# First routing and last convolution in two-bank units with a hand-placed order, and half of the casts on ScalarE

## The chip, the cores and the metric

The kernel runs on one core of one Trainium2 chip. The metric is the time of one execution on the device in microseconds (us); lower is better. The other engines are named as in the profile: PE is TensorE, PEld its weight loads, DVE is VectorE, ACT is ScalarE, POOL is GpSimd, SP the engine that issues most transfers. One run of the kernel before (547.71 us) was slow and is left out of the ratios of its job. PSUM is where this kernel's matmuls leave their results, in banks of 512 columns, and an eviction is a copy out of it by VectorE or ScalarE. A half-clock window is a stretch in which the records show a TensorE clock of 0.50.

## The reference, cut to what matters

Clustered attention feeds a gated convolution. Every key and query row is assigned to the nearest of 16 centroids of its head, a query attends only to keys of its own cluster, and the result goes through a projection into three parts, a circular convolution over the sequence (a multiplication of spectra) and an output projection.

```python
# q, k, v: (4, 8, 768, 64); centroids: (8, 16, 64)
q_assign = np.argmax(np.einsum('bhsd,hcd->bhsc', q_n, c_n), axis=-1)   # k_assign the same from k_n
mask = q_assign[:, :, :, None] == k_assign[:, :, None, :]
scores = np.where(mask, scale * np.matmul(q, k.transpose(0, 1, 3, 2)), -1e9)
attn = softmax(scores)                                   # cut: written out in the reference
x = np.matmul(attn, v).transpose(0, 2, 1, 3).reshape(4, 768, 512)
proj = x @ w_proj                                        # 512 -> 1536
x1, x2, x3 = np.split(proj, 3, axis=-1)
x2_conv = irfft(rfft(x2, axis=1) * rfft(filter_fft, axis=0), axis=1)
out = (x1 * x2_conv * x3) @ w_out
```

## The kernel before

The program has three stages.

- **Head.** The first group of four heads is loaded and transposed on PE, its similarities to the centroids are computed, and an argmax on VectorE gives one-hot rows. These are written into the operand tiles of the scores (`aug`) by small transfers. Before the first group can be used, tables of sines for the Fourier transform are built too: angles on VectorE, sines on ScalarE.
- **Loop.** 96 steps. Each step computes two score tiles on PE, two exps on ScalarE, values on PE in fp32, and two running sums on VectorE. Between these, a list called `lead` prepares the routing of the next group, and a list called `conv` runs the convolution of the batch before, one "unit" at a time.
- **Tail.** The convolution of the last batch, with no attention left to hide it.

The parts that the change touches, with cuts marked:

```python
# PSUM: eight banks. psS: two tiles of two banks, psO: one of two, psF: two of one.
def bank():                        # one bank at a time; in head and tail also halves of psS
    ...

def forward_tables(m):             # angles on VectorE, called inside routing(0) between the casts
    nc.vector.scalar_tensor_tensor(n, kc, sm, sh, op0=Alu.mult, op1=Alu.add)
    nc.vector.tensor_scalar(r, n, 1.0 / S, MAGIC, op0=Alu.mult, op1=Alu.add)
    nc.vector.tensor_scalar(r, r, MAGIC, -float(S), op0=Alu.subtract, op1=Alu.mult)
    nc.vector.tensor_tensor(n, n, r, op=Alu.add)

def tables():                      # runs as the first units of the loop
    ...                            # loads flo, fhi of the filter from ScalarE's queue
    for j in range(6):             # inverse tables: PE transposes, ScalarE copies
        ...
    nc.vector.tensor_tensor(fu, flo, fhi, op=Alu.add)
    nc.vector.tensor_tensor(fd, flo, fhi, op=Alu.subtract)
    ...                            # filter spectrum into hm, all products on VectorE

def routing(n):
    ...
    (nc.gpsimd if n else nc.vector).tensor_copy(augs[aset][0][:D, z], qf[:D])
    nc.gpsimd.tensor_copy(augs[aset][1][D:, z], qf[D:])
    if n == 0 and z:
        forward_tables(z - 1)
    ...                            # similarities, argmax, scatter

def store(self, x32):              # attention output of a pair of heads
    nc.vector.tensor_tensor(uT[:, 0, kt], x32[:, :, :64], x32[:, :, 64:], op=Alu.add)
    nc.vector.tensor_tensor(uT[:, 1, kt], x32[:, :, :64], x32[:, :, 64:], op=Alu.subtract)
    nc.gpsimd.tensor_copy(xT[:, kt], x32[:].rearrange("p t c -> p (t c)"))

def hyena(b, xT, uT, last=False):
    ...
    # convolve: one bank per half spectrum, 512 wide
    for cs in range(2):
        ps = spectrum(i, cs, uv2[:, 0], uv2[:, 1])
        for r in range(2):
            nc.vector.tensor_tensor(tm[r][:, cs], ps, hm[:, i, 2 * r + cs], op=Alu.mult)
        for r in range(2 if cs else 0):
            (nc.vector if last and r else nc.gpsimd).tensor_tensor(
                y[:, i, r], tm[r][:, 0], tm[r][:, 1], op=Alu.add)
    # invert: sum and difference on VectorE, gate product alternately on GpSimd and VectorE
    # expand: output projection, 512 wide, one transfer for two row tiles

drain(routing(0)); forward_sines()     # the sines come behind the scatter
...
while conv and paid[0] + 0.3 < due:    # fills the step with convolution units
    unit(conv)
```

The softmax here doesn't subtract the row's maximum and nothing guards it: scores larger than these inputs give would overflow.

Of the kernel before, what the change touches and what calls it, by code (L numbers as in the profile page):

```python
# [30 lines left out]
def kernel(  # L31
# [29 lines left out]


    spare = []
    more_banks = [0]

    def bank():
        if spare:
            return spare.pop(0)
        if more_banks[0]:
            more_banks[0] += 1  # L70
            if more_banks[0] % 4 in (0, 2):
                w = psS.tile([128, 2, 512], F32, name="ps")
                spare.append(w[:, 1])
                return w[:, 0]
        return psF.tile([128, 512], F32, name="pf")[:]
# [33 lines left out]
    ident = consts.tile([128, 128], F32)  # L109
    make_identity(nc, ident)  # L110
    for z in range(4):
        load_qk(0, z // 2, z % 2, (nc.sync, nc.scalar)[z % 2])
    load_v(0, 0)
    identb = consts.tile([128, 128], BF16)
    nc.vector.tensor_copy(identb, ident)
    ones32 = consts.tile([128, 32], F32)
    nc.gpsimd.memset(ones32, 1.0)

    cbd = consts.tile([128, 4, 32], F32)
    nc.gpsimd.memset(cbd, 0.0)  # L120
    cen = ctx.enter_context(tc.tile_pool(name="cen", bufs=1))
    c = cen.tile([128, D], F32)
    nc.gpsimd.dma_start(c, centroids.rearrange("h c d -> (h c) d"))
    c2 = cen.tile([128, D], F32)
    nc.vector.tensor_tensor(c2, c, c, op=Alu.mult)
    ss = cen.tile([128, 1], F32)
    nc.vector.tensor_reduce(ss, c2, axis=AX, op=Alu.add)
    nc.vector.tensor_scalar(ss, ss, 1e-30, None, op0=Alu.max)
    s0 = cen.tile([128, 1], F32)
    nc.scalar.activation(s0, ss, Act.Sqrt)  # L130

    s1 = cen.tile([128, 1], F32)
    nc.vector.reciprocal(s1, s0)
    nc.vector.tensor_tensor(s1, s1, ss, op=Alu.mult)
    nc.vector.tensor_tensor(s1, s1, s0, op=Alu.add)
    nc.vector.tensor_scalar(s1, s1, 0.5, 1e-6, op0=Alu.mult, op1=Alu.add)
    nc.vector.reciprocal(s1, s1)
    cn = cen.tile([128, D], F32)
    nc.vector.tensor_scalar(cn, c, s1, None, op0=Alu.mult)
    cps = bank()  # L140
    nc.tensor.transpose(cps[:D, :128], cn, ident)
    cv = cps[:D, :128].rearrange("d (r e c) -> d r e c", r=4, e=2)
    nc.vector.tensor_copy(cbd[:D, :, :NC], cv[:, :, 0])
    nc.vector.tensor_copy(cbd[D:, :, NC:], cv[:, :, 1])


    mka = consts.tile([128, 1], F32)
    mkb = consts.tile([128, 1], F32)
    for g in range(4):
        nc.gpsimd.memset(mka[32 * g:32 * g + 32], BIG if g % 2 == 0 else 1.0)  # L150
        nc.gpsimd.memset(mkb[32 * g:32 * g + 32], -BIG if g % 2 == 0 else 0.0)

    revc = consts.tile([128, 48, NC], BF16)
    nc.gpsimd.iota(revc, pattern=[[0, 48], [-1, NC]], base=NC, channel_multiplier=0,
                   allow_small_or_imprecise_dtypes=True)



    NSET = 2
    augs = [[consts.tile([128, 4, S], BF16, name=f"aug{i}{hp}") for hp in range(2)] for i in range(NSET)]  # L160
    nc.gpsimd.memset(augs[0][1][:D], 0.0)


    NP = 6
    pbuf = [consts.tile([128, S + 4], F32, name=f"p{i}") for i in range(NP)]
    for p in pbuf:
        nc.gpsimd.memset(p[:, S:S + 1], EPS)
    np_ = [0]

    wpj = consts.tile([128, ND, 3 * DM], BF16)  # L170
    wout = consts.tile([128, ND, DM], BF16)

# [3 lines left out]
    hw = ctx.enter_context(tc.tile_pool(name="hw", bufs=1))  # L176


    fw = [consts.tile([128, 3, HS], BF16, name=f"fw{i}") for i in range(2)]
    inv = consts.tile([128, 6, HS], BF16)  # L180
    hm = consts.tile([128, 3, 4, DM], BF16)
# [14 lines left out]
    def forward_tables(m):  # L196
        MAGIC = 12582912.0
        if m < 3:
            sm = cen.tile([128, 1], F32)
            nc.vector.tensor_scalar(sm, sq, float(2 * m), None, op0=Alu.add)  # L200
            n, r = (pbuf[2 * m + i][:, :S].rearrange("p (a b) -> p a b", a=2) for i in range(2))
            nc.vector.scalar_tensor_tensor(n, kc, sm, sh, op0=Alu.mult, op1=Alu.add)
            nc.vector.tensor_scalar(r, n, 1.0 / S, MAGIC, op0=Alu.mult, op1=Alu.add)
            nc.vector.tensor_scalar(r, r, MAGIC, -float(S), op0=Alu.subtract, op1=Alu.mult)
            nc.vector.tensor_tensor(n, n, r, op=Alu.add)

    def forward_sines():
        for m in range(3):
            n = pbuf[2 * m][:, :S].rearrange("p (a b) -> p a b", a=2)
            for i in range(2):  # L210
                nc.scalar.activation(fw[i][:, m], n[:, i], Act.Sin, scale=2.0 * math.pi / S)

    def tables():

        flo = hy.tile([128, 3, DM], F32, name="hy")
        fhi = hy.tile([128, 3, DM], F32, name="hy")
        fv = moe_filter_fft.rearrange("(w p m e) d -> w e p m d", w=2, p=64, m=3, e=2)
        for e in range(2):
            nc.scalar.dma_start(flo[64 * e:64 * e + 64], fv[0, e])
            nc.scalar.dma_start(fhi[64 * e:64 * e + 64], fv[1, e])  # L220

        for j in range(6):
# [10 lines left out]
            yield 0.3  # L233
        fu = hw.tile([128, 3, DM], BF16, name="x3", bufs=2)
        fd = hw.tile([128, 3, DM], BF16, name="x3", bufs=2)
        nc.vector.tensor_tensor(fu, flo, fhi, op=Alu.add)
        nc.vector.tensor_tensor(fd, flo, fhi, op=Alu.subtract)

        w1 = cen.tile([128, 1], F32)
        wz = cen.tile([128, 1], F32)  # L240
        wv = cen.tile([128, 1], F32)
        nc.gpsimd.memset(wz, 2.0 / S)
        nc.gpsimd.memset(wz[0:1], 0.0)
        nc.gpsimd.memset(wv, 2.0 / S)
        nc.gpsimd.memset(wv[0:1], 1.0 / S)
        nc.gpsimd.memset(w1, 0.0)
        nc.gpsimd.memset(w1[0:1], 1.0 / S)
        for i in range(3):
            for cs in range(2):
                ps = spectrum(i, cs, fu, fd)  # L250
                w = (wv, wz)[cs] if i == 0 else 2.0 / S
                nc.vector.tensor_scalar(hm[:, i, 2 * cs], ps, w, None, op0=Alu.mult)
# [8 lines left out]
            nc.vector.tensor_scalar(hm[:, i, 1], hm[:, i, 2], -1.0, None, op0=Alu.mult)  # L261

    def spectrum(i, cs, fu, fd):

        ps = bank()
# [13 lines left out]
    def routing(n):  # L279
        aset, g = n % NSET, n % 2  # L280
        qkT = {}
        for pr in range(2):
            for j in range(2):
                qr = qk_raws.pop((n, pr, j))
                z = 2 * pr + j
                qkT[z] = rt.tile([128, 2, 384], F32, name="qkT", bufs=4)
                for ch in range(2):
                    tps = bank()
                    for t in range(3):
                        nc.tensor.transpose(tps[:, ts(t, 128)],  # L290
                                            qr[:, 3 * ch + t].rearrange("p h d -> p (h d)"), ident)
                    nc.scalar.copy(qkT[z][:, ch], tps[:, :384])  # L292
                    if ch == 1:
                        load_qk(n + 1, pr, j)
                    yield 0.38
                qf = qkT[z][:].rearrange("p a b -> p (a b)")
                (nc.gpsimd if n else nc.vector).tensor_copy(augs[aset][0][:D, z], qf[:D])  # L297
                nc.gpsimd.tensor_copy(augs[aset][1][D:, z], qf[D:])
                if n == 0 and z:
                    forward_tables(z - 1)  # L300
        sim = rt.tile([128, 2, 384], F32, name="sim")
        for ch in range(2):
            sim_ps = bank()
            for z in range(4):
                nc.tensor.matmul(sim_ps[32 * z:32 * z + 32, :384], cbd[:, 2 * g + z // 2],
                                 qkT[z][:, ch], start=True, stop=True)
            nc.scalar.copy(sim[:, ch], sim_ps[:, :384])
            yield 0.75
        mx = rt.tile([128, 2, 24], F32, name="mx")
# [44 lines left out]
    class Pair:  # L354
# [110 lines left out]
        def store(self, x32):  # L465
# [3 lines left out]
            nc.gpsimd.tensor_copy(xT[:, kt], x32[:].rearrange("p t c -> p (t c)"))  # L469


    def hyena(b, xT, uT, last=False):
        uvf = uT[:].rearrange("p e k t c -> p e k (t c)")
        uv2 = hy.tile([128, 2, 3, DM], BF16, name="hy")
        y = hy.tile([128, 3, 2, DM], BF16, name="hy")
        y2 = hy.tile([128, ND, S], BF16, name="hy")
        gate = {}

        def project():
            for m in range(3):  # L480
                for e in range(2):
                    ps = bank()
                    for kt in range(ND):
                        nc.tensor.matmul(ps, uvf[:, e, kt, ts(m, 128)], wpj[:, kt, DM:2 * DM],  # L484
                                         start=(kt == 0), stop=(kt == ND - 1))
# [204 lines left out]
```

## Time and profile before

The time before is 544.42 us (median of two runs, 543.79 to 545.05). The profiled execution spans 540.5 us.

These lines are from the page of the kernel before: busy time and share of the span by engine, the granted TensorE clock in 40 slices (9 is 90% or more of full speed), and the shares of the chain that ended last.

```profile
PE 433.8 (80%) x2426; PEld 180.7 (33%) x2426; DVE 364.5 (67%) x474; ACT 257.0 (48%) x430; POOL 158.2 (29%) x154
...
PEclk9999999999999999999999979899799999898877
...
PE 46%; DVE 29%; DMA 7%; issue 7%; ACT 6%; POOL 2%; SPq 1%; ACTq 1%; DVEq 0%; POOLq 0%
```

PE is the busiest engine, but the average hides three different stages. The next view gives busy time in stretches that I chose by events in the trace: up to the first values matmul, the first 16 steps, the rest of the loop, and the last convolution. Columns: stretch, its length, then busy time and count of instructions for each engine, the granted clock, the DMA share and GB/s.

```profile
0.00:49.90 49.90, 16.68 (x73) 9.75 (x73) 22.81 (x41) 16.16 (x27) 15.05 (x39) 1.00 0.42 107
49.90:107.30 57.40, 52.05 (x340) 21.95 (x338) 45.60 (x56) 36.30 (x62) 21.42 (x25) 1.00 0.65 139
107.30:478.20 370.90, 326.06 (x1854) 133.24 (x1850) 272.43 (x342) 192.93 (x321) 114.29 (x86) 0.96 0.22 61
478.20:540.50 62.30, 39.03 (x169) 15.73 (x167) 23.68 (x36) 11.61 (x22) 7.40 (x5) 0.83 0.10 42
```

In the head and in the tail no engine is busy all the time: they are chains of handovers. In the long stretch PE is 88% busy (326.06 of 370.90).

The head in VectorE's timeline (start, duration, engine, line, operation): the third angle table stands directly in front of the argmax.

```profile
24.86 1.02 DVE L202 SCALAR_TENSOR_TENSOR p_145<-acc_174,sm,acc_175 128x768 f32<-128x768 f32 x1
...
27.98 0.55 DVE L316 TENSOR_REDUCE mx<-ps 128x24 f32<-128x384 f32 x1
```

The argmax starts at 27.98 us. The first exp is at 42.42 us. In front of it ScalarE still loads a table and computes the six sines, until 41.11 us, and loads the exp table:

```profile
37.23 1.28 ACT L211 ACT_TABLE_LOAD   x1 [16.40 <-DMA aug_137<-ohT]
...
42.42 0.81 ACT L369 ACTIVATE p_141<-ps 128x768 f32<-128x768 f32 x1
```

In the loop, these lines of GpSimd, VectorE and PE show a chain. GpSimd casts; two of VectorE's adds beside them take 1.57 us where later ones take 0.95; VectorE comes late to a gate product (L513); PE waits 4.23 us for it (in brackets: the idle time before, and what ended it). The two slow adds are 1.2 us of this lateness; the rest is the other work in VectorE's queue in front of the product, mostly the argmax.

```profile
308.03 1.14 POOL L297 CAST aug_136<-qkT 64x768 bf16<-64x768 f32 x1
309.23 1.44 POOL L298 CAST aug_137<-qkT 64x768 bf16<-64x768 f32 x1
```

```profile
308.41 1.57 DVE L387 TENSOR_TENSOR acc_2487<-acc_2487,p_143 128x768 f32<-128x768 f32 x1
309.90 1.57 DVE L387 TENSOR_TENSOR acc_2488<-acc_2488,p_144 128x768 f32<-128x768 f32 x1
...
313.51 0.95 DVE L387 TENSOR_TENSOR acc_2487<-acc_2487,p_145 128x768 f32<-128x768 f32 x1
...
317.69 0.55 DVE L513 TENSOR_TENSOR x_2593<-pf,x_2593 128x384 f32<-128x384 f32 x1
```

```profile
318.30 1.87 PE L526 MATMUL pf<-inv,hy 128*128 128x384 bf16 x7 [4.23 <-DVE x_2593 L513]
```

The tail in PE's timeline: the fourth half-spectrum waits 3.83 us for VectorE's products of the one before, and gates and spectra alternate with waits for banks.

```profile
490.55 0.81 PE L268 MATMUL ps<-hy,fw_168 128*128 128x512 bf16 x3
495.19 1.08 PE L268 MATMUL ps<-hy,fw_168 128*128 128x512 bf16 x3 [3.83 <-DVE tm L495]
...
501.34 0.81 PE L508 MATMUL ps<-xT,wpj 128*128 128x384 bf16 x4 [2.37 <-DVE tm L495]
```

### The profile page before, as it was taken

What the parts mean: (1) busy time and instruction counts of PE and PEld (TensorE: products, weight loads), DVE (VectorE), ACT (ScalarE), POOL (GpSimd) and SP (SyncE); (2) the same over time, 40 slices, a digit from 0 to 9 for tenths busy, and PEclk for the clock granted to TensorE, in tenths of its full rate; (3) what the DMA queues carried; (4) which work ended last, traced back from release to release, by engine and by line L of the source; (5) the groups of instructions that cost most, each with busy time, mean ns of one, the idle gap of its engine ahead of it and who ended that gap; (6) DMA issues with size and microseconds to landing.
All of it is one profiled execution on the core that took longest, in us unless ns stands there. A gap on an engine that the chain in (4) does not pass through costs nothing.

```text
span 540.5 us, 6748 instructions
## 1 busy us (share of the span) xinstructions
PE 433.8 (80%) x2426; PEld 180.7 (33%) x2426; DVE 364.5 (67%) x474; ACT 257.0 (48%) x430; POOL 158.2 (29%) x154
## 2 busy tenths in 40 slices
PE   2515889989997898999998969798698898585755
PEld 1203334434432333433433414342243343232311
DVE  2941787998988878776777965748366968317441
ACT  3226447857753465566665625365365364150211
POOL 6401600802603652235106710242101522101020
PEclk9999999999999999999999979899799999898877
DMA  8324772705501340235224302020140000020002
GB/s 206 87 58 116 145 145 66 179 24 148 119 17 44 88 118 2 60 89 158 79 60 117 90 0 60 4 86 0 40 138 2 30 3 29 2 116 0 1 0 116
DMA packets 67304, 38.42 MB, mean 71 GB/s; under 512 B 55932, under 2 KB 62520, under 8 KB 67272
## 3 DMA queue, kind: packets, MB, share of 16 engines
q1 hardware_dynamic: 62088, 33.42, 22.4%
q0 software_dynamic: 1088, 2.13, 2.2%
q10 hardware_dynamic: 4096, 2.46, 2.0%
q8 instruction: 19, 0.31, 0.2%
q14 instruction: 13, 0.11, 0.1%
HBM read 32.04 MB, written 7.85 MB: 74 GB/s over the span
## 4 chain that ended last, share of the span: by engine, by line
PE 46%; DVE 29%; DMA 7%; issue 7%; ACT 6%; POOL 2%; SPq 1%; ACTq 1%; DVEq 0%; POOLq 0%
PE o L380 14%; PE ps L365 7%; PE pf L508 4%; DVE tm L495 4%; PE pf L547 4%; DMA rb<-dr 3%; PE pf L402 3%; PE pf L526 2%; PE pf L484 2%; PE pf L290 2%; DVE uT L468 2%; PE ps L508 2%; DMA hy<-in_moe_filter_fft_dram 2%; DVE cand L317 1%; POOL hy L536 1%
## 5 line engine op out<-in xcount | busy, mean ns | idle before, releaser
L497 POOL TENSOR_TENSOR hy<-tm 128x512 bf16<-128x512 f32 x21 | 30.6, 1474 | 69.3 <-DVE tm L495 69.3
L380 PE MATMUL o<-p_141,vraw 128*64 128x385 f32 (+1 forms) x128 | 50.1, 515 | 0.4 <-ACT osb L394 0.4
L380 PE MATMUL o<-p_142,vraw 128*64 128x385 f32 (+1 forms) x128 | 50.1, 515 | 0.0
L508 PE MATMUL pf<-xT,wpj 128*128 128x384 bf16 x212 | 43.9, 333 | 7.0 <-DVE yy L535 2.8
L380 PE MATMUL o<-p_143,vraw 128*64 128x385 f32 (+1 forms) x128 | 49.4, 509 | 0.0
L380 PE MATMUL o<-p_144,vraw 128*64 128x385 f32 (+1 forms) x128 | 49.4, 509 | 0.0
L380 PE MATMUL o<-p_146,vraw 128*64 128x385 f32 (+1 forms) x128 | 48.6, 503 | 0.0
L380 PE MATMUL o<-p_145,vraw 128*64 128x385 f32 (+1 forms) x128 | 48.6, 503 | 0.0
L369 ACT ACTIVATE p_141<-ps 128x768 f32<-128x768 f32 x32 | 26.0, 811 | 44.9 <-PE ps L365 36.9
L369 ACT ACTIVATE p_145<-ps 128x768 f32<-128x768 f32 x32 | 26.0, 812 | 31.1 <-PE ps L365 21.3
L369 ACT ACTIVATE p_143<-ps 128x768 f32<-128x768 f32 x32 | 26.2, 819 | 23.5 <-PE ps L365 23.5
L508 PEld LDWEIGHTS <-wpj 128*128 128x128 bf16 x256 | 25.1, 100 | 33.3 <-issue 17.3
L297 POOL CAST aug_138<-qkT 64x768 bf16<-64x768 f32 x16 | 18.0, 1125 | 57.4 <-ACT qkT L292 57.2
L495 DVE TENSOR_TENSOR tm<-pf,hm 128x512 f32<-128x512 f32 x40 | 25.2, 676 | 10.3 <-PE pf L268 7.1
L290 PE MATMUL pf<-ident,qkraw 128*128 128x128 f32 x171 | 29.8, 284 | 2.1 <-ACT qkT L292 1.0
L547 PE MATMUL pf<-wout,hy 128*128 128x512 bf16 x80 | 23.4, 425 | 9.1 <-POOL hy L536 8.6
L526 PE MATMUL pf<-inv,hy 128*128 128x384 bf16 (+1 forms) x108 | 21.8, 349 | 9.8 <-DVE x_2593 L513 4.2
L292 ACT COPY qkT<-pf 128x384 f32<-128x384 f32 x57 | 27.7, 486 | 2.9 <-PE pf L290 2.9
L369 ACT ACTIVATE p_142<-ps 128x768 f32<-128x768 f32 x32 | 26.1, 815 | 6.0 <-PE ps L365 5.7
L365 PE MATMUL ps<-aug_137 128*128 128x384 bf16 x96 | 24.2, 334 | 5.5 <-ACT p_141 L369 5.5
L365 PE MATMUL ps<-aug_136 80*128 80x384 bf16 x96 | 24.6, 339 | 4.3 <-DMA aug_137<-ohT 3.4
L369 ACT ACTIVATE p_144<-ps 128x768 f32<-128x768 f32 x32 | 26.4, 826 | 2.2 <-PE ps L365 2.0
(507 smaller groups left out, 1000.1 us busy)
## 6 DMA issues: line engine op xcount, KB each, us to landing
qkraw<-in_q_dram SPq DMA_DIRECT2D x32, 192.0 KB
vraw<-in_v_dram SPq DMA_DIRECT2D x8, 768.0 KB
out_dram<-tm SPq DMA_DIRECT2D x12, 512.0 KB
rb<-dr SPq DMA_DIRECT2D x30, 192.0 KB
qkraw<-in_k_dram SPq DMA_DIRECT2D x28, 192.0 KB
hy<-in_moe_filter_fft_dram ACTq DMA_DIRECT2D x4, 384.0 KB
wpj<-in_moe_w_proj_dram POOLq DMA_DIRECT2D x1, 1536.0 KB, 11.3
od<-ohT SPq DMA_DIRECT2D x7, 192.0 KB
```

What stands on the lines that cost most here:

```text
L290: nc.tensor.transpose(tps[:, ts(t, 128)], qr[:, 3 * ch + t].rearrange("p h d -> p (h d)"), ident)
L292: nc.scalar.copy(qkT[z][:, ch], tps[:, :384])
L297: (nc.gpsimd if n else nc.vector).tensor_copy(augs[aset][0][:D, z], qf[:D])
L365: nc.tensor.matmul(sps[:, ch, :384], self.aug[hp][:K, 2 * self.pr + 1, ts(sk, 128)], self.aug[hp][:K, 2 * self.pr, ts(ch, 384)], start=Tru ...
L369: nc.scalar.activation(p[:, :S].rearrange("p (a b) -> p a b", a=2), sps[:, :, :384], Act.Exp, scale=0.125)
L380: nc.tensor.matmul(self.o[64 * hp:64 * hp + 64, ch, :384 + ch], vv[:, 2 * self.pr + hp, sk * D:(sk + 1) * D], pb[hp][sk][:, 384 * ch:384 * ...
L402: nc.tensor.matmul(dps[32 * z:32 * z + 32, :384], ones32, self.acc[hp][:, ts(ch, 384)], start=True, stop=True)
L495: nc.vector.tensor_tensor(tm[r][:, cs], ps, hm[:, i, 2 * r + cs], op=Alu.mult)
L497: (nc.vector if last and r else nc.gpsimd).tensor_tensor(y[:, i, r], tm[r][:, 0], tm[r][:, 1], op=Alu.add)
L508: nc.tensor.matmul(ps[:, :384], wpj[:, kt, off + dt * 128:off + dt * 128 + 128], xT[:, kt, ts(ch, 384)], start=(kt == 0), stop=(kt == ND - 1))
L526: nc.tensor.matmul((pe, po)[e][:, :384], y[lo:hi, i, cs, ts(dt, 128)], inv[lo:hi, row], start=(n == 0), stop=(n == 3))
L547: nc.tensor.matmul(ps, y2[:, kt, ts(2 * tt + e, 128)], wout[:, kt], start=(kt == 0), stop=(kt == ND - 1))
```

## The change

The intent: shorten the two chains that nothing hides, and relieve GpSimd. The angle tables move in front of the first routing, the sines beside the argmax, the inverse tables out of the loop into the wait for the scatter, and the filter is loaded early. The first routing and the last convolution take two PSUM banks at a time from three double buffers, so that evictions are twice as wide. In the loop, the casts of one half of the heads' rows (28) and of the attention output (16) go from GpSimd to ScalarE. Smaller parts: the filter's sum and difference go from VectorE to GpSimd, three of the five products of the filter's spectrum to ScalarE, GpSimd's adds in the loop's convolutions are issued 1.5 us later in program order, and a convolution unit of zero cost now ends the filling of a step (a pause).

```diff
+    def banks():                       # two banks, from three double buffers in turn
+        turn[0] += 1
+        if turn[0] % 3:
+            return psS.tile([128, 2, 512], F32, name="ps")
+        return psO.tile([128, 2, 512], F32, name="o")
...
+    for e in range(2):                 # filter loaded at the start, SP's queue
+        nc.sync.dma_start(flo[64 * e:64 * e + 64], fv[0, e])
+        nc.sync.dma_start(fhi[64 * e:64 * e + 64], fv[1, e])
...
-        nc.vector.tensor_tensor(fu, flo, fhi, op=Alu.add)
-        nc.vector.tensor_tensor(fd, flo, fhi, op=Alu.subtract)
+        nc.gpsimd.tensor_tensor(fu, flo, fhi, op=Alu.add)
+        nc.gpsimd.tensor_tensor(fd, flo, fhi, op=Alu.subtract)
...
-                (nc.gpsimd if n else nc.vector).tensor_copy(augs[aset][0][:D, z], qf[:D])
+            if n == 0:
+                nc.vector.tensor_copy(augs[aset][0][:D, z], qf[:D])
+            else:
+                later(0.8, lambda z=z, qf=qf: nc.scalar.copy(augs[aset][0][:D, z], qf[:D]))
...
+        if n == 0:
+            sines()                    # between similarities and argmax
...
-            nc.gpsimd.tensor_copy(xT[:, kt], x32[:].rearrange("p t c -> p (t c)"))
+            nc.scalar.copy(xT[:, kt], x32[:].rearrange("p t c -> p (t c)"))
...
+        def alone(self):               # the last convolution
+            for i in range(3):
+                gate(i)                # two double-bank units
+                ps = banks()
+                for cs in range(2):
+                    spectrum(i, cs, self.uv2[:, 0], self.uv2[:, 1], ps[:, cs])
+                for r in range(2):
+                    tm = hw.tile([128, 2, DM], F32, name="tm", bufs=3)
+                    nc.vector.tensor_tensor(tm, ps, hm[:, i, 2 * r:2 * r + 2], op=Alu.mult)
+                    nc.gpsimd.tensor_tensor(self.y[:, i, r], tm[:, 0], tm[:, 1], op=Alu.add)
...
+    angles(1)
+    angles(2)
     drain(routing(0))
+    inverse_tables()
...
-        while conv and paid[0] + 0.3 < due:
-            unit(conv)
+        while conv and paid[0] + 0.3 < due and unit(conv):
+            pass
```

## The prediction

> What bounds the kernel now. The page gives TensorE 433.8 of 540.5 us busy, VectorE 364.5, ScalarE 257, GpSimd 158; the chain of waits is 46% TensorE and 29% VectorE. The stages differ. Head (timeline): first scores at 37.0 us, first exp at 42.4, first values matmul at 49.9. Loop (42 to 464 us): TensorE about 89% busy, so close to bound. Tail (478.2 to 540.5 us, the last convolution alone): TensorE about 60% busy, ended by PSUM handovers and VectorE.
>
> Head, on the critical path. VectorE runs three angle tables (about 3.2 us each) until 28.0 before the argmax, though the transposed similarities were ready at 22.4. Then come 5 us of argmax, 0.9 of transposes and a 2.6 us scatter; the six sines with their table load (37.2 to 41.1) and the exp table load (1.28) still stand before the first exp. With angles run during the loads and sines beside the argmax, I expect similarities at about 22, scores at 31, and the six inverse-table copies (0.48 each) inside the scatter wait and just after it: first exp at about 35.5, 7 us earlier. The first two steps also lose their stalls (inverse-table copies behind filter loads on ScalarE; VectorE waiting 6.3 us for the filter, landed at 57.6). First values at about 39: 11 us earlier, kept through the first dozen steps. Estimate: -12.
>
> Tail, all critical. Before, projection to first inverse takes 478.2 to 513.7. With double banks, three deep: projection 24 matmuls of 0.215 = 5.2 us; four gate units of 2.6; three spectra of 1.3, paced by VectorE's two 1024-wide multiplies and one gate multiply (about 3.3 to 4 us per turn), since the second add (1.25) goes to GpSimd. First inverse at about 499.6: -14. The join chain (VectorE add and subtract 1.1, GpSimd product 1.8, one yy buffer) stays about 11 us. The expansion saves bank waits and half of the last output transfer: -2. Together -16. The Trainium skill (TensorE: Matmul & The Clock Gate, Part 1) has the clock halve after about 3.4 us of idleness; the trace agrees (clock 0.50 from 519.5 to 533.1, after idling from 517.2), and I expect this to remain in the expansion.
>
> Loop. GpSimd loses 28 aug casts (33 us) and 16 xT casts (19 us). The skill (SBUF, Who interferes with whom) says that VectorE with two SBUF inputs contends with GpSimd's reads. The trace agrees: accumulations of 0.87 us take up to 1.57 beside casts; summed excess of VectorE over each form's shortest is 51 us in the loop, about a quarter beside these casts. Gain on the chain about 5. The pauses before the expansion spare some of the 8.6 us in which TensorE waited for GpSimd's product. Against: ScalarE gains 44 copies of about 0.8 us (35), where it is already 75 to 80% busy (90 to 110 us), and the xT copy waits in ScalarE's queue for VectorE, which waits for broadcasts (18.7 us in nine waits); exps behind it slip. Net -3, from -12 to +10.
>
> Total 544.4 - 12 - 16 - 3 = 513 us. Range 502 to 526.
>
> Right if: first exp near 35 us; last convolution near 46 us instead of 62; VectorE accumulations shorter; ScalarE busy near 290. Wrong if ScalarE's idle shows long waits on the VectorE line before xT copies, with TensorE idle and more half-clock windows in the loop; if the early filter transfers delay the first q and k; or if GpSimd's adds (now six in the tail) end the waits before the inverse.
>
> Chances: faster 0.93, same 0.05, slower 0.02.

## The result, and the profile after

The changed kernel takes 506.95 us (median of two runs, 505.48 to 508.41), 37.5 us less. The ratio is 0.9312 (95% interval 0.9187 to 0.9436). Ratios here are the mean time of one kernel's fast runs over that of the other's of the same rounds, so they are not quite the ratio of the medians that are quoted. Where runs of different jobs are compared below, the difference of their ratios is multiplied by 544 us. A repeat with six runs gave 504.91 us and 0.9292 (0.9261 to 0.9323).

The same lines of the page after:

```profile
PE 424.1 (84%) x2426; PEld 181.0 (36%) x2426; DVE 342.1 (68%) x451; ACT 286.3 (57%) x470; POOL 115.3 (23%) x116
...
PEclk9999999999999899999999997989989999998987
...
PE 52%; DVE 22%; DMA 8%; ACT 7%; issue 5%; SPq 2%; POOL 2%; POOLq 0%; ACTq 0%; DVEq 0%
```

And the four stretches, cut at the same events:

```profile
0.00:46.50 46.50, 18.70 (x96) 12.04 (x96) 30.88 (x40) 17.25 (x28) 23.50 (x49) 1.00 0.59 141
46.50:98.70 52.20, 50.13 (x318) 20.85 (x317) 38.10 (x47) 43.20 (x72) 9.03 (x10) 1.00 0.61 134
98.70:459.50 360.80, 321.73 (x1853) 133.12 (x1850) 252.95 (x340) 216.39 (x357) 71.61 (x50) 0.97 0.22 62
459.50:503.60 44.10, 33.52 (x169) 14.96 (x167) 20.21 (x24) 9.48 (x14) 11.11 (x8) 0.88 0.15 59
```

The second column against that of before is the account of the gain: head -3.4, first 16 steps -5.2, rest of the loop -10.1, tail -18.2, together -36.9 us of span. VectorE's work in the long stretch fell from 272.43 to 252.95 us with two instructions fewer.

The head is the surprise. VectorE is busier in it than before, 30.88 us. Its timeline and GpSimd's show why:

```profile
17.86 2.15 DVE L307 CAST aug_167<-qkT 64x768 bf16<-64x768 f32 x1
...
20.39 7.48 DVE L307 CAST aug_167<-qkT 64x768 bf16<-64x768 f32 x3
27.80 0.54 DVE L330 TENSOR_REDUCE mx<-pf 128x24 f32<-128x384 f32 x1
```

```profile
16.79 2.80 POOL L647 MEMSET aug_170<- 64x3072 bf16 x1
19.67 3.62 POOL L248 TENSOR_TENSOR x_395<-hy 128x1536 bf16<-128x1536 f32 x1
23.25 3.74 POOL L249 TENSOR_TENSOR x_396<-hy 128x1536 bf16<-128x1536 f32 x1
```

The angles are out of the way, but three casts that take 0.54 to 1.18 us each in the kernel before now take 7.48 us together. The raw records give 3.31, 3.77 and 0.54 us; the two long ones end at 23.70 and 27.40 us, 0.41 us after GpSimd's two sums. The argmax starts at 27.80 us, as before, and the first exp is at 41.78 us instead of 42.42.

The sines, which now run beside the argmax, no longer stand in front of the first exp, but this brings only 0.6 us, because the six copies of the inverse tables have taken their place. They start when ScalarE has issued its scatter transfers, and end at 40.17 us:

```profile
37.17 0.86 ACT L242 COPY inv<-pf 128x384 bf16<-128x384 bf16 x2 [9.43 <-DMA aug_168<-ohT]
...
41.78 0.81 ACT L383 ACTIVATE p_134<-ps 128x768 f32<-128x768 f32 x1
```

The tail shows what it was built for. From the first projection to the first inverse PE's timeline shows no wait at all (one spectrum is shown, without a bracket); the first one is short, in the inverses, for GpSimd's add:

```profile
471.20 1.46 PE L276 MATMUL ps<-hy,fw_141 128*128 128x512 bf16 x6
...
479.21 1.08 PE L513 MATMUL ps<-inv,hy 128*128 128x384 bf16 x6
480.64 1.52 PE L513 MATMUL ps<-inv,hy 64*128 64x384 bf16 x10 [0.35 <-POOL hy L616]
...
489.64 0.61 PE L518 MATMUL ps<-wout,hy 128*128 128x512 bf16 x1 [2.40 <-POOL hy L531]
...
493.79 3.40 PE L518 MATMUL o<-wout,hy 128*128 128x512 bf16 x8
```

The first inverse starts 19.7 us after the first projection (479.21 - 459.50); before it was 35.5 (513.67 - 478.20). The expansion (L518) still runs slowly: eight matmuls in 3.40 us, in a recorded half-clock window from 486.6 to 496.8 us.

ScalarE does wait in front of the moved attention-output cast. The trace lists the idle time before line 483 by what ended it; one of the two largest entries (us, times) is:

```profile
DVE x_2737 L447: 4.1, 1
```

In all there are ten waits of 26.6 us. Whether they cost anything is a question for an experiment.

### The profile page after: what moved, and what is told of

It is laid out like the page before. It is cut to its first block, busy times and chain, and to the rows that moved or that the text cites. A ratio compares the mean times of both kernels' runs of the same rounds, so it can differ in the third digit from the quotient of the medians.

```text
span 503.6 us, 6673 instructions
## 1 busy us (share of the span) xinstructions
PE 424.1 (84%) x2426; PEld 181.0 (36%) x2426; DVE 342.1 (68%) x451; ACT 286.3 (57%) x470; POOL 115.3 (23%) x116
## 4 chain that ended last, share of the span: by engine, by line
PE 52%; DVE 22%; DMA 8%; ACT 7%; issue 5%; SPq 2%; POOL 2%; POOLq 0%; ACTq 0%; DVEq 0%
PE o L394 17%; PE ps L379 9%; PE pf L501 4%; DMA rb<-dr 4%; PE pf L518 3%; PE pf L496 3%; PE pf L416 3%; DVE tm L546 3%; PE pf L297 2%; PE pf L513 2%; DVE aug_167 L307 2%; DMA dr<-dn 2%; DMA dn<-dd 2%; DVE acc_3389 L401 1%; SPq L101 1%
## 5 line engine op out<-in xcount | busy, mean ns | idle before, releaser
L549 POOL TENSOR_TENSOR hy<-tm 128x512 bf16<-128x512 f32 x18 | 26.8, 1509 | 98.1 <-DVE tm L546 98.1
L501 PE MATMUL pf<-xT,wpj 128*128 128x384 bf16 x192 | 39.5, 334 | 7.5 <-DVE yy L530 4.5
L383 ACT ACTIVATE p_134<-ps 128x768 f32<-128x768 f32 x32 | 26.0, 812 | 25.7 <-PE ps L379 19.6
L383 ACT ACTIVATE p_138<-ps 128x768 f32<-128x768 f32 x32 | 26.0, 813 | 20.2 <-PE ps L379 18.6
L310 POOL CAST aug_170<-qkT 64x768 bf16<-64x768 f32 x16 | 16.1, 1004 | 93.5 <-ACT qkT L299 93.5
L383 ACT ACTIVATE p_136<-ps 128x768 f32<-128x768 f32 x32 | 26.3, 823 | 15.7 <-PE ps L379 15.7
L546 DVE TENSOR_TENSOR tm<-pf,hm 128x512 f32<-128x512 f32 x36 | 22.6, 678 | 11.4 <-PE pf L276 8.1
L310 POOL CAST aug_168<-qkT 64x768 bf16<-64x768 f32 x16 | 17.2, 1079 | 47.9 <-ACT qkT L299 45.0
L383 ACT ACTIVATE p_135<-ps 128x768 f32<-128x768 f32 x32 | 26.1, 814 | 2.8 <-PE ps L379 2.7
L383 ACT ACTIVATE p_137<-ps 128x768 f32<-128x768 f32 x32 | 26.5, 829 | 0.2 <-PE ps L379 0.2
L383 ACT ACTIVATE p_139<-ps 128x768 f32<-128x768 f32 x32 | 26.0, 813 | 0.5 <-PE ps L379 0.5
L297 PEld LDWEIGHTS pf<-ident,qkraw 128*128 128x128 f32 x168 | 21.7, 147 | 12.7 <-ACT qkT L299 4.5
```

Of the source, the lines that this page charges most:

```text
L297: nc.tensor.transpose(tps[:, ts(t, 128)], qr[:, 3 * ch + t].rearrange("p h d -> p (h d)"), ident)
L383: nc.scalar.activation(p[:, :S].rearrange("p (a b) -> p a b", a=2), sps[:, :, :384], Act.Exp, scale=0.125)
L501: nc.tensor.matmul(ps, wpj[:, kt, off + dt * 128:off + dt * 128 + 128], self.xT[:, kt, ts(ch, 384)], start=(kt == 0), stop=(kt == ND - 1))
L549: nc.gpsimd.tensor_tensor(self.y[:, i, r], tm[r][:, 0], tm[r][:, 1], op=Alu.add)
```

## The experiments

My theory after reading the result: the tail is worth about 18 us by itself; the loop gained because VectorE is less held up by GpSimd; the head's expected gain was given back to a new collision of the same kind. Rivals: the head was bound by something else; the loop's gain came from pauses, later adds or tables; the ScalarE queue loses what VectorE gains. Twelve kernels were run, each with six runs, and all gave correct results. The intervals of the ratios are about 0.003 to 0.004 to either side, so a difference of two of them is known to about 2 to 3 us; a smaller one is not clear of noise.

### The changed kernel again

> The changed kernel again, to have its spread on the chip of the next runs. Two runs so far: 505.5 and 508.4 us. Expected 503 to 510 us, about 37 us under the kernel before, the spread going with the number of half-clock windows of TensorE.

Measured 504.91 us (504.1 to 507.06), ratio 0.9292. The base for the runs of the same job is therefore known to about 0.3%. That the spread goes with the clock is not borne out: the fastest run (504.1 us) had a mean clock of 0.949, the run with the highest (0.973) took 505.16 us, and the two slowest had 0.942 and 0.943.

### Filter sums back on VectorE

```diff
-        nc.gpsimd.tensor_tensor(fu, flo, fhi, op=Alu.add)
-        nc.gpsimd.tensor_tensor(fd, flo, fhi, op=Alu.subtract)
+        nc.vector.tensor_tensor(fu, flo, fhi, op=Alu.add)
+        nc.vector.tensor_tensor(fd, flo, fhi, op=Alu.subtract)
```

> Only the two 1536-wide filter sums go back from GpSimd to VectorE, behind the argmax in its queue. Theory A (in the head the gain was given back: the sums on GpSimd block VectorE's three casts, 7.48 us for three instead of about 0.55 us each, and the argmax starts at 27.8 us as it did before): the three casts take under 2.5 us together, the argmax starts before 24.5 us, the first exp moves from 41.8 to about 37 us, and the time falls by 3 to 5 us. Rival B (the argmax waits for the similarities or their transposes in any case): the first exp stays within 1 us of 41.8 and the time within 1 us.

Measured 501.06 us, ratio 0.9209 (0.9182 to 0.9237) against 0.9292 for the changed kernel in the same job: 3.9 us faster. VectorE's timeline of this run:

```profile
17.86 2.14 DVE L307 CAST aug<-qkT 64x768 bf16<-64x768 f32 x1
...
20.39 1.49 DVE L307 CAST aug<-qkT 64x768 bf16<-64x768 f32 x3
24.17 0.56 DVE L330 TENSOR_REDUCE mx<-pf 128x24 f32<-128x384 f32 x1 [2.29 <-PE pf L328]
...
30.61 1.75 DVE L248 TENSOR_TENSOR x<-hy 128x1536 bf16<-128x1536 f32 x1
```

The three casts take 1.49 us, the argmax starts 3.6 us earlier and now waits for the transposed similarities, and the first exp is at 38.17 us. The sums take 1.75 us each on VectorE at a time when it has nothing else to do. Theory A holds; the collision is shown by taking it away. The first cast still takes 2.14 us beside GpSimd's clearing of a tile, and the similarities start only at 20.5 us because the centroid tile is copied behind it, and behind the angle tables, which end at 17.9 us: so not all of the expected 7 us were lost to the sums.

### The old tail

The method `alone` is replaced by the last convolution of the kernel before, written for the new class: single banks from the same pools and in the same order.

```diff
-                ps = banks()
-                for cs in range(2):
-                    spectrum(i, cs, self.uv2[:, 0], self.uv2[:, 1], ps[:, cs])
+                for cs in range(2):
+                    ps = spectrum(i, cs, uv2[:, 0], uv2[:, 1])      # one bank
+                    for r in range(2):
+                        nc.vector.tensor_tensor(tm[r][:, cs], ps, hm[:, i, 2 * r + cs], op=Alu.mult)
...
```

> The changed kernel with the last convolution of the kernel before (single-bank units, every other sum on VectorE, whole output transfers). Theory: the new tail is worth about 18 us by itself (44.1 instead of 62.3 us from its first projection), nothing else moves: 523 to 526 us. Rival: the tail of the changed kernel is shorter partly because GpSimd or the clock arrive in a better state from the loop: under 519 us.

Measured 523.61 us, ratio 0.9622 against 0.9292: the new tail is worth 18 us (0.0330 of 544). The theory holds, and the rival falls. In the profiles the last convolution takes 59.6 us here, against 44.0 in the changed kernel of the same job, but 62.3 in the kernel before. Half-clock windows cover 11 us of it here and 21 in the kernel before, so some of the 18.2 us that the first pair of profiles shows may be clock. Which part of the new tail (double banks, order, adds on GpSimd, split output transfers) brings how much was not tried.

### Both moved casts back on GpSimd

```diff
-                later(0.8, lambda z=z, qf=qf: nc.scalar.copy(augs[aset][0][:D, z], qf[:D]))
+                nc.gpsimd.tensor_copy(augs[aset][0][:D, z], qf[:D])
...
-            nc.scalar.copy(xT[:, kt], x32[:].rearrange("p t c -> p (t c)"))
+            nc.gpsimd.tensor_copy(xT[:, kt], x32[:].rearrange("p t c -> p (t c)"))
```

> Both moved casts (28 of the heads' rows, 16 of the attention output) go back from ScalarE to GpSimd, all else as changed. Theory A (the loop gained 10 us between 84.6 us and the tail mostly because GpSimd no longer holds up VectorE's two-input adds; excess of VectorE in the loop 51 us before, 39 after): the excess goes back to about 50 us and the time rises by 4 to 8 us. Rival B (the loop's gain comes from the pauses, the deferred adds or the tables): excess may rise, time within 2 us. Rival C (ScalarE's queue pays more than VectorE gains): the time falls.

Measured 510.55 us, ratio 0.9387 against 0.9292: 5.2 us slower. VectorE's excess in the loop (each instruction's duration less the shortest of its line and shape in the same run, summed) is 52.3 us against 40.2 in the changed kernel of the same job. The running sums alone are quick to check: their busy time in the loop, in the windows view restricted to their line, is 178.18 us for 160 adds before, 167.91 after, and 180.74 here:

```profile
42.00:464.00 422.00, 178.18 (x160) 0.97 0.28 72
```

```profile
42.00:448.00 406.00, 167.91 (x160) 0.98 0.27 71
```

```profile
42.00:454.00 412.00, 180.74 (x160) 0.96 0.27 70
```

(The columns are the stretch, its length, VectorE's busy time with the count, clock, DMA share, GB/s.) Theory A holds for about half of the long stretch's gain: it takes 365.9 us here, between 370.9 and 360.8. Half-clock windows cover 27.3 us of this stretch before, 20.5 after and 27.3 here. Since work at half clock takes at most twice as long, this can be up to 3.4 us of the difference; whether the casts act partly through the clock was not separated.

### Only the attention-output casts back

> Only the 16 casts of the attention output (xT) go back from ScalarE to GpSimd. Both moved casts together were worth 5.6 us (510.6 against 504.9). Theory of the prediction (the xT copy holds up ScalarE's queue, 27 us of idle in front of ten of them in the changed kernel, so that one was a loss): the time falls by 1 to 3 us. Rival (its hold-up costs nothing, VectorE's relief counts): it rises by 1 to 3 us.

Measured 505.4 us, ratio 0.929 (0.9257 to 0.9322), against 0.9292 of the changed kernel in the job before. Both statements miss: moving these 16 casts to ScalarE neither gains nor loses. VectorE's excess stays at 40.6 us, but here this measure is blind. The second of the two sums in `store` (L482) runs beside the cast in all 16 cases when GpSimd casts, so the shortest of them is slow too. Its durations (shortest, median, longest, in ns), in the changed kernel run again and in this run:

```profile
L482 DVE TENSOR_TENSOR uT<-x x16: 546/551/1178, 87.4 to 454.1; 128x384 bf16<-128x384 f32 x16
```

```profile
L482 DVE TENSOR_TENSOR uT<-x x16: 1172/1176/1179, 87.5 to 455.0; 128x384 bf16<-128x384 f32 x16
```

The 16 take 9.4 us together there and 18.8 here. So the move does relieve VectorE, by about 9 us, and it does make ScalarE wait; the time shows neither. Whether the two cancel or both lie off the critical path was not separated. By difference, the casts' gain in time is that of the 28 casts of the heads' rows; these were not moved back alone.

### No pauses

```diff
-        while conv and paid[0] + 0.3 < due and unit(conv):
-            pass
+        while conv and paid[0] + 0.3 < due:
+            unit(conv)
```

> Only the pauses are undone: the filling loop again runs through units of zero cost. Theory (the pauses spare TensorE waits for GpSimd's product in front of the expansion, 8.6 us in three before): the waits of the expansion's matmuls on GpSimd come back, the time rises by 2 to 6 us. Rival (the pauses only shift work): within 1.5 us.

Measured 507.02 us, ratio 0.9325 (0.9283 to 0.9367), 1.8 us above the changed kernel's ratio with intervals that overlap. PE's waits for GpSimd's product before the expansion do come back:

```profile
PE pf L518 <- POOL hy L531: 6.0, 2, 5.5
```

This says 6.0 us in two waits, the longest 5.5; the changed kernel has 2.3 us in one, and the kernel before had 8.6 us in three. The mechanism is seen, its worth is not clear of noise: the profiled run of this kernel spans 503.3 us, as long as that of the changed kernel.

### Adds at once

> Only GpSimd's adds of the loop's convolutions are again issued right behind the products instead of 1.5 us later in program order. GpSimd is 23% busy and its queue has little behind it, so I expect less than 1.5 us either way; a rise of over 2 us would say that the order on GpSimd carried part of the loop's gain.

Measured 506.34 us, ratio 0.9308 (0.9269 to 0.9346): 0.9 us above, not clear of noise, as expected.

### The loop's part undone as a whole

All three edits above together: casts, pauses and adds as in the kernel before.

> Both casts back on GpSimd, no pauses, adds at once: the loop's part of the change undone as a whole, head and tail as changed. In the profiles the stretch from the 17th step's values to the last convolution took 370.9 us before, 360.8 changed, 365.9 with only the casts undone. Theory A (casts, pauses and adds make up the whole gain of this stretch, the last two only where VectorE is late): the stretch goes to 369 to 372 us, the time to 513 to 517. Rival B (the rest of 5 us is drift of half-clock windows and phase): the stretch stays at 365 to 367, the time at 509 to 512.

Measured 514.45 us, ratio 0.9448 (0.9413 to 0.9482), 8.5 us above the changed kernel's ratio. The long stretch takes 369.3 us in the profile, against 370.9 before. Both are inside the ranges of theory A. Casts account for 5.2 us of this; pauses and adds share the other 3.3 (known to about 2.5), and how they share it stays open. Rival B is not wholly excluded: half-clock windows cover 30.7 us of the stretch here against 20.5 in the changed kernel, so up to 5 us may come by way of the clock.

### Only the casts moved, in the kernel before

> The other way round: the kernel before with only the two moved casts (28 rows of the heads, 16 of the attention output on ScalarE). Theory A (moved casts are worth 5 to 6 us by themselves): 538 to 540 us, VectorE's excess in the loop from 51 to about 40 us. Rival (they pay only together with the pauses and deferred adds): within 2 us of the kernel before.

Measured 536.81 us, ratio 0.9851 (0.9808 to 0.9895): 8 us faster than the kernel before (the interval excludes 1), the excess of VectorE in the loop down from 50.5 to 36.8 us. The casts pay by themselves, and the rival falls. That they pay more here than in the changed kernel (8 against 5.2 us) is not clear of noise; the time lies a microsecond below my range.

### The filter loaded late

On top of the version with the sums on VectorE, the four filter loads go back to ScalarE's queue behind the first exps.

> The version with the filter sums on VectorE (501.1 us), but with the filter loaded late, from ScalarE's queue behind the first exps, as the kernel before does. Theory (the early load is what shortened the first 17 steps, 57.4 to 52.2 us, and the wait before the first values): VectorE waits 5 us or more for the filter, first exp unchanged at 38.2, the first 17 steps take 54 to 58 us, the time rises to 504 to 507 us. Rival (inverse tables out of the loop did it): the steps stay near 52 us and the time within 1.5 us of 501.1.

Measured 516.34 us, ratio 0.9502 (0.9462 to 0.9543), against 0.9209: 16 us slower. The first exp is still at 38.2 us, but the first values come at 55.2 us instead of 42.9. VectorE:

```profile
30.00 0.68 DVE L347 TENSOR_SCALAR ohT<-pf,mka,mkb 128x768 bf16<-128x768 bf16 x1 [0.99 <-PE pf L345]
51.96 1.76 DVE L248 TENSOR_TENSOR x<-hy 128x1536 bf16<-128x1536 f32 x1 [21.28 <-DMA hy<-in_moe_filter_fft_dram]
```

Neither statement holds as a whole. The 16 steps take 53.2 us, nearly unchanged, as the rival said: the early load is not what shortened them. But the time rises by far more than either allowed, and the loss is in front of the first values. The reason is in the order of units. In the kernel before, six inverse-table units stood in `conv` in front of the filter's spectrum and covered the load. With these moved into the head, the first unit in PE's queue is the spectrum, and the values stand behind it: PE waits 12.02 us for VectorE's sum, which waits for the filter. In this order of units the early load is a condition for moving the inverse tables. The profile accounts for 10.7 us of span of the 16 (510.9 against 500.2); the profiled run was the fastest of the six, the others took 515.9 to 519.2 us, and what made them longer I can't say.

### A version built on this

Head: the filter sums on VectorE; the second and third angle tables behind the centroid copy; GpSimd's clearing of the second tile two steps into the loop; an exp of one column behind the sines, so that its table is loaded early; inverse tables in three double-bank units; only two of the eight scatter transfers on ScalarE's queue; one filter product back on VectorE. Tail: a second buffer for the sum and difference, and separate output tiles.

```diff
+        early = cen.tile([128, 1], F32)
+        nc.scalar.activation(early, sq, Act.Exp, scale=0.0)
...
             if n == 0 and z == 0:
                 spread_centroids()
+            if n == 0 and z < 2:
+                angles(z + 1)
...
-            yy = hw.tile([128, NT, 128], F32, name="yy")
+            yy = (at if dt % 2 and own else hw).tile([128, NT, 128], F32, name="x32" if dt % 2 and own else "yy")
```

> A version built on what the runs showed. Head: filter sums on VectorE behind the argmax; the second angle tables after the centroids are spread, so that the similarities need not wait for them; GpSimd's clearing of the second set 2 steps later; the exp table loaded early; inverse tables in three double banks; only the first pair's scatter on ScalarE's queue; the negated filter column on VectorE. Tail: a second buffer for the sum and difference before the gate product, outputs in separate tiles. Expected: first exp near 30 to 33 us (41.8 in the changed kernel, 38.2 with the sums on VectorE), last convolution about 40 us instead of 44: 490 to 496 us. If steps after the first exp are bound by ScalarE, part is given back and it ends near 498.

Measured 493.16 us, ratio 0.9059 (0.9025 to 0.9092). The argmax starts at 20.75 us, the first exp is at 30.91 us, the first values at 35.7 instead of 46.5, and the last convolution takes 40.5 us instead of 44.1. This is within what was expected. It was measured as a whole; its single edits were not separated.

### The same with TensorE kept busy

Twenty matmuls whose result nobody reads fill PE's wait before the expansion.

```diff
+            fill = bank()
+            for k_ in range(20):
+                nc.tensor.matmul(fill, wout[:, 0, :128], wout[:, 1], start=True, stop=True)
```

> The improved version (493.2 us) with 20 idle matmuls of 512 columns into an unused bank between the last inverse and the expansion, 4.3 us at full clock. Their result is not used. Theory (the expansion runs at half clock because TensorE idled before it: 8 matmuls took 3.4 to 3.6 us of time where they take 1.9 at full clock): the half-clock window before the expansion goes, the expansion ends 1.5 to 3 us earlier, 490 to 492 us. Rival (output copies and transfers end the time): no change; or the filler delays the expansion and the time rises.

Measured 490.75 us, ratio 0.9012 (0.898 to 0.9044), 2.6 us below the version without filler by ratios of two jobs. PE's timelines of the two, without and with filler:

```profile
480.51 3.55 PE L525 MATMUL o<-wout,hy 128*128 128x512 bf16 x8
483.89 1.89 PE L525 MATMUL ps<-wout,hy 128*128 128x512 bf16 x8
```

```profile
473.43 4.26 PE L634 MATMUL pf<-wout 128*128 128x512 bf16 x19 [0.16 <-issue]
477.53 1.89 PE L525 MATMUL ps<-wout,hy 128*128 128x512 bf16 x8
479.26 1.89 PE L525 MATMUL o<-wout,hy 128*128 128x512 bf16 x8
480.99 1.89 PE L525 MATMUL ps<-wout,hy 128*128 128x512 bf16 x8
```

All three groups of eight now take 1.89 us. Of the profiled difference in span of 2.8 us, only 1.2 lies in the tail (39.3 against 40.5 us); the rest arose before it. That the filler keeps the clock up is shown; the gain of 1 to 3 us is small and, with intervals that overlap, hardly clear of noise. At 490.75 us this is the fastest kernel, 54 us under the kernel before.

## Why the prediction was right or wrong

The prediction was 513 us with a range of 502 to 526; the result was 506.95. The direction and the range were right. The terms of the sum were not equally good, and that the total is only 6 us off is partly luck: in the profiles the head brought 3.4 us less than predicted, the tail 2.2 and the loop 7.1 more.

- **Tail: predicted -16, measured -18.2 in the profile and -18 by the experiment.** The mechanism was right in that the new tail, with its double banks, has no PE waits up to the first inverse, and that the join chain behind them hardly changes (10.1 us against 11.1). What paces the spectra was not: the prediction had VectorE's multiplies set turns of 3.3 to 4 us, but a turn is 3.90 us of PE's own work (spectra start at 467.30 and 471.20 without a wait between), and VectorE, with 3.3 us of work in it, waits for PE. The first inverse was predicted 21.4 us after the first projection (499.6 - 478.2) and came after 19.7. The half clock in the expansion was predicted and is there (486.6 to 496.8 us). The page "TensorE: Matmul & The Clock Gate" of the Trainium skill (Part 1) says that the clock halves after about 3.4 us of idleness and comes back under load. The clock records here agree in part: there are only values of 0.50 and 1.00, in windows of 3.4 us and multiples, and the filler removes the window in the expansion. But full idleness was not needed. In the 3.41 us before the window at 486.6 us PE was busy 51% of the time, with 1.19 us as its longest wait, and in the kernel before PE had been idle for only 2.2 us (from 517.3) when the clock fell at 519.5.
- **Head and first steps: predicted -12, measured -8.6 (3.4 before the first values, 5.2 in the next 16 steps).** The step that failed is the prediction's "first exp at about 35.5, 7 us earlier". It came 0.6 us earlier. I had costed each moved instruction in isolation and had not asked what GpSimd's queue, now ahead of its time because the filter arrives early, would run against. GpSimd's sums of 3.62 and 3.74 us fell on VectorE's casts. With the sums elsewhere the first exp is at 38.17; with the order of the head mended as well, at 30.91. So the sums are 3.6 of the 6.3 us by which the first exp missed 35.5. Another 2.2 us can be read from the trace of that run: the transposed similarities were ready at about 24.2 us, not at 22, because the centroid copy stood behind the angle tables and a slow cast. The copies of the inverse tables in front of the first exp were in the prediction and took about what it gave them. The first values still came 3.4 us earlier: before, the first inverse-table copy stood in ScalarE's queue behind four filter loads that it issued (46.5 to 49.1 us in the trace); after, the copies are done in the head. This part was read from the traces, not tried alone.
- **Loop: predicted -3 with -12 to +10, measured -10.1 in the profile for the long stretch, and 8.5 us when its three edits were undone.** The mis-sized term is the net of gain and loss. The gain on VectorE's chain was put at 5; undoing the casts cost 5.2, and this is gain and loss together. The loss that I set against it, "the xT copy waits in ScalarE's queue for VectorE", exists as a wait, 26.6 us in ten, but it is no net loss: with the copy back on GpSimd the time is the same. And the pauses with the deferred adds brought about 3 us more.
- **ScalarE near 290 us busy**: 286.3. **VectorE's additions shorter**: 167.91 us for 160 against 178.18. Both as predicted.
- **Half-clock windows**: they became fewer, 30.5 us within the profiled span against 48.3, not more. They vary from run to run of the same kernel (mean clock 0.942 to 0.973 in six runs), so no part of the gain is claimed for them; as said above, some of it may pass through them.

The contention itself is as the page "SBUF — State Buffer" of the Trainium skill has it (Who interferes with whom): a VectorE instruction with two inputs in SBUF contends with a GpSimd instruction that reads SBUF, and copies and casts of VectorE can use the shared ports too, where the one that comes second waits for the whole instruction. The trace agrees: adds of 0.95 us at 1.57 beside casts, and casts of 0.55 us at 3.31 and 3.77 us, ending 0.41 us after GpSimd's instructions of 3.62 and 3.74 us. The prediction used this rule for the loop and did not apply it to the head.

## What to carry to other kernels

When work is moved to an idle engine, ask when that engine will run it, not only how long it takes: an engine with an empty queue starts as soon as its inputs are there (GpSimd's sums started at 19.67 us, right behind the clearing of a tile), and if it shares a path to memory with the engine on the critical path, the move can cost more there than it saves. In a chain that nothing hides, look for handovers: here the tail that takes two banks at a time from three double buffers was worth 18 us. A wait that a profile shows in a queue is not yet a cost, and relief of an engine is not yet a gain: undo the one instruction and look at the time. And an excess over the shortest instance misses an instruction that is hindered every time.

## What the Trainium skill lacked or had wrong

- "ScalarE: Activation LUTs" (What ACT_TABLE_LOAD costs) gives about 2.66 us for a switch of tables, 1.28 of load and 1.38 of drain. Here only the load appears: in the changed kernel the load starts at 23.85 us, 0.02 us after the copy before it ends (23.35 + 0.48), takes 1.28 us, and the first sine starts at 25.14 us. The exp table in the improved version, from 20.89 to 22.18 us, is the same.
- "SBUF — State Buffer" (Who interferes with whom) says that the order of issue decides who blocks, and gives slowdowns of 6.8 and 1.5 times. What this costs a whole kernel is missing: two casts of 0.55 us took 3.31 and 3.77 us, and putting the GpSimd sums elsewhere was worth 3.9 us of a kernel of 505.
- "TensorE: Matmul & The Clock Gate" (Part 1) advises against idle gaps of more than about 3.4 us. Here shorter ones were enough: half-clock windows began after 3.41 us in which PE was busy 51% (at 486.6 us, longest wait 1.19 us) and 35% (at 519.5 us in the kernel before). The page has no figure for filling a gap with unread matmuls. Here 20 of 512 columns kept the clock at full rate, and the groups of eight matmuls that follow took 1.89 us instead of up to 3.55; the kernel gained 1 to 3 us, hardly clear of noise.
